# A scan kernel's first four steps: unit 1's state sums copied right behind step 0's k, and pieces of the weights taken up one place sooner

## The chip, the cores and the metric

One core of a Trainium2 chip runs the whole program. The metric is the device time in microseconds from the first to the last instruction; a profile of the same kernel has a span of its own, some tenths of a percent shorter. TensorE, VectorE, ScalarE, GpSimd and SyncE each work through a queue of their own in the order in which the program lists their instructions; semaphores hold an instruction back until what it needs is done. SyncE's queue issues nearly all transfers.

## The reference

A Mamba-2 scan is followed by a gated feed-forward block:

```python
# x: 4 sequences, 8 heads, 768 tokens, 32 wide; a: a decay per token; B, C: 16 wide
for c in range(nc):                       # chunks of the sequence
    L = exp(cum[:, :, :, None] - cum[:, :, None, :]) * causal
    y_intra = einsum('bhij,bhjd->bhid', einsum('bhin,bhjn->bhij', Cc, Bc) * L, xc)
    y_inter = einsum('bhin,bhnd->bhid', Cc, state) * exp(cum)[..., None]
    y[:, :, sl] = y_intra + y_inter
    state = decay_full * state + einsum('bhjn,bhjd->bhnd', Bc * decay_from_j, xc)
# y as (3072 tokens, 256)
h = y @ w_in            # 256 -> 2048
g = h * cos(h)
out = g @ w_out         # 2048 -> 256
```

The weights arrive as 64-bit floats and are used as 32-bit ones, so the kernel first puts the two 32-bit words of each number together.

## The kernel before, in words

The kernel cuts the sequences into chunks of 128 tokens (`NC` is 6). For each chunk it computes the scan's `y`, keeps it transposed in `yT`, and runs the feed-forward block over it in 16 steps (`NF`), each for 512 columns of hidden values: tokens of a part of the chunk by two groups of 128 hidden features. Chunk 0 is handled in two units of 64 tokens of every sequence, so that the first feed-forward steps can begin as soon as unit 0's `y` is there; step n of chunk 0 belongs to unit n mod 2.

A step consists of these pieces, each a short function:

- `first(n)` (L650): 8 matmuls of TensorE, `hp` from `w_in` and `yT`, into one PSUM bank. They are L663 in the profile.
- `wind_k(n)`: ScalarE rounds `hp`/2π to the integer `k` (L670). `wind_w(n)`: VectorE takes `w = hp/2π - k` (L676). `wind` is both.
- `gate(n)`: ScalarE turns `w` into the cosine (L685).
- `gated(n)`: VectorE multiplies `hp` by it into `gT` (L690); this is the last reader of `hp(n)`.
- `second(n)`: 8 matmuls of TensorE in chunk 0, `gT` by `w_out` into the accumulators `o` (L734).

The weights come in 16 pieces, `("in", 0..7)` and `("out", 0..7)`, each 512 KB of words. `grade` takes one up: ScalarE takes the absolute value of the high words (L231), GpSimd clamps it (L232), and ScalarE scales the low words (L229, the function `rest`, which with `later=True` is handed back and called afterwards). `join` finishes it: two VectorE instructions (L244, L246) and an addition on GpSimd (L254) that writes the piece into `w_in` or `w_out`. The tiles `mag` and `last` that lie between have three buffers each, the words eight. Steps 0 and 1 use pieces in 0 and out 0; steps 2 and 3 use in 1 and out 1; steps 4 and 5 use in 2 and out 2; steps 6 and 7 use in 3 and out 3.

The order on every engine is written out by hand. `first_steps` (L929) lists the steps 0 to 3 of chunk 0 along with the end of the scan of unit 1; from step 4 on, a loop does it: `first(n)`, `wind(n)`, the next piece's `grade`, `gate(n)`, the due `join`, `gated(n)`, parts of the next chunk's scan, and then `second(n - 2)`. The scan of the next chunk puts decay scans on VectorE (L510), one each in the steps 4, 6, 8 and 9; they read `arow`, a row of decays spread over all partitions by a DMA. `clips` computes what these DMAs read (`a_cut`, `a_all`), and SyncE's loads of chunk 1 come behind its two transfers.

PSUM, the accumulators' memory, is divided by tags with two buffers each: `"h"` and `"o"` of one bank, and `"scan"` of a pair of banks. A buffer goes to a new tile only when all readers of the old one are done. Chunk 0's scan uses `"scan"` for its matrices; `finish0(1)`, which runs in the middle of `first(0)`, takes both of them for unit 1's `y`. From each, ScalarE copies 256 columns of every partition to `yT` (L466). The first, `y[0]`, also holds unit 1's sums for the next state in other columns. The function `take_s1` copies these to `state` in two ScalarE instructions (L476); `add_s1`, at step 6, adds the old state to them on GpSimd. The steps 2 and 3 have `tag=None`, which means that their `hp` lies in a buffer of the tag `"scan"` (L652); the steps 0, 1 and those from 4 on use the tag `"h"`.

Of the kernel before, what the change touches and what calls it, by code (L numbers as in the profile page):

```python
# [25 lines left out]
def kernel(  # L26
# [42 lines left out]
    def bank(shape, name, tag):  # L69
        return psum.tile(shape, FP32, tag=tag, bufs=2, name=name)  # L70

    def pair(name):

        return psum.tile([P, 2, 4 * P], FP32, tag="scan", bufs=2, name=name)
# [120 lines left out]
    def kept(which, i):  # L195
        return (w_in[:, :, i * WC:(i + 1) * WC] if which == "in" else
                w_out[:, i * WF:(i + 1) * WF])
# [14 lines left out]
    def shares(which, ap, n):  # L212

        return [ap] if n == 1 else [ap.rearrange("p (k e f) -> p e k f", k=KT, e=n)[:, e]
                                    for e in range(n)]

    def grade(which, i, later=False, n=1):


        t = words.pop((which, i), None)  # L220
        if t is None:
            return
        mag = conv.tile([P, 2 * WC], FP32, tag="mag", bufs=3, name="mag")
        last = conv.tile([P, 2 * WC], U32, tag="last", bufs=3, name="last")
        low, high, mags, lasts = (shares(which, ap, n) for ap in (t[:, :, 0], t[:, :, 1], mag, last))
        held[which, i] = list(zip(high, shares(which, mag.bitcast(U32), n), lasts))

        def rest(e=0):
            ACT.activation(lasts[e], low[e], AF.Copy, scale=2.0 ** -29)  # L229
        for e in range(n):  # L230
            ACT.activation(mags[e], high[e].bitcast(FP32), AF.Abs)  # L231
            G.tensor_scalar(out=mags[e], in0=mags[e], scalar1=MOST, scalar2=LEAST,  # L232
                            op0=ALU.min, op1=ALU.max)
            if not later:
                rest(e)
        if later:
            return rest

    def join(which, i):


        parts = held.pop((which, i), ())
        for e, (high, bits, last) in enumerate(parts):
            V.tensor_scalar(out=bits, in0=bits, scalar1=3, scalar2=0x3FFFFFFF,  # L244
                            op0=ALU.logical_shift_left, op1=ALU.bitwise_and)
            V.scalar_tensor_tensor(out=bits, in0=high, scalar=0xC0000000, in1=bits,  # L246
                                   op0=ALU.bitwise_and, op1=ALU.bitwise_or)
            dst = kept(which, i)
            if len(parts) > 1:
                dst = dst[:, :, e * P:(e + 1) * P]  # L250
            else:
                bits, last = (ap.rearrange("p (k f) -> p k f", k=dst.shape[1])
                              for ap in (bits, last))
            G.tensor_tensor(out=dst.bitcast(U32), in0=bits, in1=last, op=ALU.add)  # L254
# [10 lines left out]
    for s in range(2):  # L265
# [3 lines left out]
        out=a_in, in_=a.rearrange("(u b) h (c p) -> (b h c) u p", u=NU, p=P))  # L269
# [91 lines left out]
    def weigh0(k):  # L361
        scs[k] = sc = scan.tile([P, 2 * H, N], FP32, tag="sc0", bufs=1, name="sc0")
        G.tensor_tensor(out=sc, in0=bs[:, k].rearrange("p q (h n) -> p (q h) n", h=H),
                        in1=lams[k].rearrange("p q h i -> p (q h) i")[:, :, W - 1:W]
                        .to_broadcast([P, 2 * H, N]), op=ALU.mult)
# [53 lines left out]
    def weights(k, q):  # L419

        m_of[k] = units[k]
        m, l = (ap[:, :, HH * q:HH * (q + 1)].rearrange("p s (k t) i -> p k s (t i)", k=2)
                for ap in (units[k], lams[k]))
        V.tensor_tensor(out=m, in0=gs[k, q][:, :, 0:2 * P].rearrange("p k (s i) -> p k s i", s=2),
                        in1=l, op=ALU.mult)
# [219 lines left out]
    def turn_of(n):  # L645

        c, f = divmod(n, NF)
        return (f % 2, f // 2) if c == 0 else divmod(f, NJ)

    def first(n, between=None, tag="h"):  # L650
        c, f = divmod(n, NF)
        hp[n] = bank([P, TB], "hp", tag) if tag else pair("hp")[:, 0]  # L652

        u, j = turn_of(n)
        if c == 0:
            to_, y = hp[n].rearrange("p (e i) -> p e i", e=2), yT[0][:, u]
        else:
            to_ = hp[n].rearrange("p (e t s i) -> p e t s i", e=2, t=2, s=2)
            y = yT[c].rearrange("p k (u s t i) -> p k u t s i", u=2, s=2, t=2)[:, :, u]
        for e in range(2):  # L660
            fs = slice((2 * j + e) * P, (2 * j + e + 1) * P)
            for k in range(KT):
                PE.matmul(to_[:, e], lhsT=w_in[:, k, fs], rhs=y[:, k],  # L663
                          start=(k == 0), stop=(k == KT - 1), skip_group_check=True)
            if between and e == 0:
                between()

    def wind_k(n):
        k = ffn.tile([P, TB], I32, tag="k", name="k")
        ACT.activation(k, hp[n], AF.Copy, bias=0.25, scale=INV_2PI)  # L670
        turns[n] = k

    def wind_w(n):
        k = turns[n]
        turns[n] = w = ffn.tile([P, TB], FP32, tag="w", name="w")
        V.scalar_tensor_tensor(out=w, in0=hp[n], scalar=INV_2PI, in1=k,  # L676
                               op0=ALU.mult, op1=ALU.subtract)

    def wind(n):
        wind_k(n)  # L680
        wind_w(n)

    def gate(n):
        cos = turns[n]
        ACT.activation(cos, cos, AF.Sin, bias=quarter, scale=TWO_PI)  # L685

    def gated(n):
        cos = turns.pop(n)
        gT[n] = ffn.tile([P, TB], FP32, tag="gT", bufs=LAG + 1, name="gT")
        V.tensor_tensor(out=gT[n], in0=hp.pop(n), in1=cos, op=ALU.mult)  # L690
        gT[n] = gT[n].rearrange("p (q m) -> p q m", q=4)
        if NF <= n < NC * NF - 1:
            differ(n)
# [29 lines left out]
    def second(n):  # L723
        c, f = divmod(n, NF)
        if c > 0:
            seven(n)
            return
        u, j = turn_of(n)
        if j == 0:
            o[c, u] = bank([P, 2, DM], "o", "o")  # L730
        g = gT.pop(n)
        for e in range(2):
            for t in range(2):
                PE.matmul(o[c, u][:, t], lhsT=g[:, 2 * e + t], rhs=w_out[:, 2 * j + e],  # L734
                          start=(j == e == t == 0), stop=(j == NJ - 1 and e == 1),
                          skip_group_check=True)
        if j < NJ - 1:
            return
        ob = conv.tile([P, 2, DM], FP32, tag="last", bufs=3, name="ob")
        ACT.copy(out=ob, in_=o[c, u])  # L740
        for p in range(2):
            nc.sync.dma_start(out=unit_rows[p, u], in_=ob[p * W:(p + 1) * W])
# [124 lines left out]
    def units_of_decay():  # L867
        G.tensor_copy(out=unit[:, 0:HH * P].rearrange("p (h i) -> p h i", h=HH),
                      in_=ident.unsqueeze(1).to_broadcast([P, HH, P]))
        G.tensor_copy(out=unit[:, HH * P:], in_=ident[:, 0:W])  # L870

    def clips():
        G.tensor_scalar(out=cut, in0=a_in, **clip)
        G.memset(cut[:, :, 0:1], 0.0)
        G.tensor_scalar(out=la, in0=a_in, **clip)
        for dst, src in ((a_cut, cut), (a_all, la)):
            nc.sync.dma_start(
                out=dst.rearrange("(u b) h (c p) -> (b h c) u p", u=NU, p=P), in_=src)
# [50 lines left out]
    def first_steps():  # L929

        weigh0(1)
        grade("in", 1)
        units_of_decay()
        for q in range(2):
            weights(1, q)
        states_of = []
        first(0, lambda: states_of.extend(finish0(1)))
        take_s1, add_s1 = states_of
        join("in", 1)
        wind(0)  # L940
        first(1)
        rest = grade("out", 0, later=True)
        clips()
        gate(0)
        rest()
        join("out", 0)
        gated(0)
        first(2, tag=None)
        wind(1)
        rest = grade("in", 2, later=True)  # L950
        gate(1)
        rest()
        join("in", 2)
        gated(1)
        first(3, tag=None)
        wind(2)
        rest = grade("out", 1, later=True)
        gate(2)
        rest()
        join("out", 1)  # L960
        second(0)
        gated(2)
        wind(3)
        second(1)
        rest = grade("in", 3, later=True)
        gate(3)
        take_s1()
        rest()
        join("in", 3)
        gated(3)  # L970
        grade("out", 2)
        return add_s1

    add_s1 = first_steps()
# [86 lines left out]
```

## Time and profile before

| | |
|---|---|
| time | 381.97 us, median of 3 runs (381.56 to 382.55) |
| span of the profile | 380.6 us, granted TensorE clock 0.990 |
| TensorE | 366.1 us busy, 96% of the span |
| VectorE | 280.3 us, 74% |
| GpSimd | 215.0 us, 56% |
| ScalarE | 172.6 us, 45% |
| data moved | 31.55 MB, 83 GB/s on average; 218 to 299 GB/s between 9.5 and 47.5 us |

In the digits of the profile's page each place is a fortieth of the span, 9.5 us; a digit is the busy share in tenths, and the row PEclk gives the clock that TensorE was granted, in tenths of full speed. In the timeline a line has its start in us, its length in us, engine, line of the code, operation, the tiles written and read, and the number of instructions that it merges; in brackets stands the idle time before it with what ended it. "issue" there means that nothing the profile shows held the engine back. `first_steps` takes place between 13 and 37 us; step 4 follows.

### The profile page before, as it was taken

How to read it: one execution, taken by the hardware profiler on the slowest of the kernel's cores; microseconds unless marked ns; L12 is line 12 of the kernel's file. 1: busy time of each engine (PE TensorE's matmuls, PEld its weight loads, DVE VectorE, ACT ScalarE, POOL GpSimd, SP SyncE). 2: the span in 40 equal slices, each digit the busy share in tenths (PEclk: the TensorE clock that was granted, in tenths of full speed). 3: DMA queues.
4: the chain of work that ended last, by engine and by line, in shares of the span. 5: the costliest groups of instructions: out<-in, count | busy, mean ns of one | idle time of the engine just before them, and what ended most of it. 6: DMA issues, size and time to landing. Idle time of an engine off the chain costs nothing.

```text
span 380.6 us, 8692 instructions
## 1 busy us (share of the span) xinstructions
PE 366.1 (96%) x3276; PEld 327.9 (86%) x3276; DVE 280.3 (74%) x471; ACT 172.6 (45%) x293; POOL 215.0 (56%) x334
## 2 busy tenths in 40 slices
PE   8929999999999999999999999999999999999996
PEld 4628887888989899999989999989999999999995
DVE  7672899989979966987775887875888782554543
ACT  3564666535335334434433444443444443434442
POOL 6563486459974553684354776344666434444551
PEclk9996999999999999999999999999999999999999
DMA  9988987315425732664222745121020010010011
GB/s 144 299 221 218 251 203 144 80 15 146 108 61 85 133 80 44 83 154 110 42 53 24 131 106 125 22 43 16 4 37 11 0 30 2 0 29 2 0 30 28
DMA packets 121354, 31.55 MB, mean 83 GB/s; under 512 B 90496, under 2 KB 117216, under 8 KB 121312
## 3 DMA queue, kind: packets, MB, share of 16 engines
q1 hardware_dynamic: 119024, 30.54, 37.4%
q10 hardware_dynamic: 2288, 0.46, 0.6%
q8 instruction: 26, 0.43, 0.5%
q14 instruction: 16, 0.13, 0.1%
HBM read 27.64 MB, written 3.34 MB: 81 GB/s over the span
## 4 chain that ended last, share of the span: by engine, by line
PE 78%; SPq 5%; DVE 5%; POOL 5%; DMA 3%; issue 2%; ACT 1%; POOLq 0%; ACTq 0%
PE hp L663 37%; PE o L772 30%; SPq L110 4%; PE y L602 3%; PE o L734 2%; PE g L560 2%; POOL words L709 2%; DMA bc<-in_C_dram 1%; PE y L595 1%; DMA arow<-a_cut 1%; DVE mag L246 1%; DVE gT L690 1%; DVE w L676 1%; DVE mag L244 1%; POOL gd L715 1%
## 5 line engine op out<-in xcount | busy, mean ns | idle before, releaser
L663 PE MATMUL hp<-yT,w_in 128*128 128x256 f32 x768 | 185.4, 385 | 8.2 <-DVE gT L690 6.2
L663 PEld LDWEIGHTS hp<-yT,w_in 128*128 128x128 f32 x768 | 140.5, 192 | 28.3 <-issue 10.8
L715 POOL TENSOR_TENSOR gd<-gT 128x256 f32<-128x256 f32 x79 | 59.0, 747 | 98.8 <-DVE gT L690 93.0
L685 ACT ACTIVATE w<-w,quarter 128x512 f32<-128x512 f32 x96 | 69.2, 721 | 77.5 <-DVE w L676 77.5
L676 DVE SCALAR_TENSOR_TENSOR w<-hp,k 128x512 f32<-128x512 f32 x96 | 65.4, 682 | 47.4 <-ACT k L670 47.3
L670 ACT ACTIVATE k<-hp 128x512 int32<-128x512 f32 x96 | 57.2, 596 | 89.7 <-PE hp L663 89.5
L690 DVE TENSOR_TENSOR gT<-hp,w 128x512 f32<-128x512 f32 x96 | 65.2, 679 | 33.0 <-ACT w L685 24.1
L772 PE MATMUL o<-words,gd 128*128 128x128 f32 x474 | 65.8, 275 | 0.0
L772 PEld LDWEIGHTS o<-words,gd 128*128 128x128 f32 x474 | 59.3, 192 | 0.0
L510 DVE TENSOR_TENSOR_SCAN lam<-arow,unit 128x512 f32<-128x512 f32 x40 | 56.5, 1411 | 0.0
L772 PEld LDWEIGHTS o<-w_out,gT 128*128 128x128 f32 x316 | 47.5, 191 | 4.0
L718 POOL TENSOR_TENSOR gd<-gT,gd 128x128 f32<-128x128 f32 x79 | 44.6, 565 | 6.2
L772 PE MATMUL o<-w_out,gT 128*128 128x128 f32 x316 | 48.0, 274 | 0.0
L717 POOL TENSOR_TENSOR gd<-gT,gd 128x128 f32<-128x128 f32 x79 | 44.0, 557 | 6.2
L734 PE MATMUL o<-w_out,gT 128*128 128x256 f32 x128 | 31.3, 390 | 0.0
L581 DVE TENSOR_TENSOR m<-g,lam 128x256 f32<-128x256 f32 x80 | 30.9, 415 | 0.5
L772 PE MATMUL o<-w_out,gd 128*128 128x128 f32 x158 | 30.6, 275 | 0.0
L772 PE MATMUL o<-words,gT 128*128 128x128 f32 x158 | 30.5, 275 | 0.0
L734 PEld LDWEIGHTS o<-w_out,gT 128*128 128x128 f32 x128 | 25.3, 198 | 3.7
L772 PEld LDWEIGHTS o<-w_out,gd 128*128 128x128 f32 x158 | 24.0, 192 | 0.0
L772 PEld LDWEIGHTS o<-words,gT 128*128 128x128 f32 x158 | 24.0, 192 | 0.0
L232 POOL TENSOR_SCALAR mag<-mag 128x512 f32<-128x512 f32 x16 | 11.6, 726 | 11.1 <-ACT mag L231 11.0
(108 smaller groups left out, 269.1 us busy)
## 6 DMA issues: line engine op xcount, KB each, us to landing
arow<-a_cut SPq DMA_DIRECT2D x20, 512.0 KB
words<-in_moe_w_in_dram SPq DMA_DIRECT2D x8, 512.0 KB
words<-in_moe_w_out_dram SPq DMA_DIRECT2D x8, 512.0 KB
out_dram<-sum SPq DMA_DIRECT2D x18, 128.0 KB
blocks<-in_B_dram SPq DMA_DIRECT2D x128, 8.0 KB
blocks<-in_C_dram SPq DMA_DIRECT2D x128, 8.0 KB
xr<-in_x_dram SPq DMA_DIRECT2D x14, 128.0 KB
along<-a_all SPq DMA_DIRECT2D x20, 64.0 KB
```

Of the source, the lines that this page charges most:

```text
L510: V.tensor_tensor_scan(out=lam[c, b][:, hs].rearrange("p h i -> p (h i)"), data0=rows_.rearrange("p h i -> p (h i)"), data1=unit[:, b % 2 ...
L581: V.tensor_tensor(out=m_[js, :, :, is_], in0=g_[js, :, :, is_], in1=l_[js, :, :, is_], op=ALU.mult)
L663: PE.matmul(to_[:, e], lhsT=w_in[:, k, fs], rhs=y[:, k], start=(k == 0), stop=(k == KT - 1), skip_group_check=True)
L670: ACT.activation(k, hp[n], AF.Copy, bias=0.25, scale=INV_2PI)
L676: V.scalar_tensor_tensor(out=w, in0=hp[n], scalar=INV_2PI, in1=k, op0=ALU.mult, op1=ALU.subtract)
L685: ACT.activation(cos, cos, AF.Sin, bias=quarter, scale=TWO_PI)
L690: V.tensor_tensor(out=gT[n], in0=hp.pop(n), in1=cos, op=ALU.mult)
L715: G.tensor_tensor(out=d[:, 0:2], in0=g[:, 1:2].to_broadcast([P, 2, P]), in1=g[:, 3::-3], op=ALU.subtract)
L717: G.tensor_tensor(out=d[:, 2], in0=g[:, 0], in1=d[:, 0], op=ALU.subtract)
L718: G.tensor_tensor(out=d[:, 3], in0=g[:, 2], in1=d[:, 2], op=ALU.subtract)
L734: PE.matmul(o[c, u][:, t], lhsT=g[:, 2 * e + t], rhs=w_out[:, 2 * j + e], start=(j == e == t == 0), stop=(j == NJ - 1 and e == 1), skip_gr ...
L772: PE.matmul(at[q], lhsT=a_[q], rhs=w[q], start=(j == 0 and q in starts), stop=(j == NJ - 1), skip_group_check=True)
```

## The change

The change rewrites the order inside `first_steps` and nothing else; no instruction is added or removed. It has four parts.

1. `take_s1()` moves from behind `gate(3)` to right behind step 0's `wind_k`, so that the buffer with the state sums becomes free before the steps 2 and 3 ask for theirs.
2. Each piece of weights from out 0 to out 2 is taken up one place sooner: out 0 ahead of `first(0)` instead of behind `first(1)`, in 2 in step 0 instead of step 1, and so on; out 2, which was taken up at the end of `first_steps`, is taken up in step 3.
3. The joins of out 0 and out 1 move up: out 0's two VectorE instructions stand between `wind_k(0)` and `wind_w(0)`, out 1's between `first(3)` and `wind(2)`. Those of in 2 and in 3 stay where they were.
4. `clips()` comes behind `gate(0)` instead of ahead of it; on GpSimd it now follows the clamp of in 2 instead of that of out 0.

```diff
+        rest = grade("out", 0, later=True)
         states_of = []
         first(0, lambda: states_of.extend(finish0(1)))
         take_s1, add_s1 = states_of
+        rest()
         join("in", 1)
-        wind(0)
+        wind_k(0)
+        take_s1()
+        join("out", 0)
+        wind_w(0)
         first(1)
-        rest = grade("out", 0, later=True)
+        rest = grade("in", 2, later=True)
+        gate(0)
         clips()
-        gate(0)
         rest()
-        join("out", 0)
         gated(0)
         first(2, tag=None)
         wind(1)
-        rest = grade("in", 2, later=True)
+        rest = grade("out", 1, later=True)
         gate(1)
         rest()
         join("in", 2)
         gated(1)
         first(3, tag=None)
+        join("out", 1)
         wind(2)
-        rest = grade("out", 1, later=True)
+        rest = grade("in", 3, later=True)
         gate(2)
         rest()
-        join("out", 1)
         second(0)
         gated(2)
         wind(3)
         second(1)
-        rest = grade("in", 3, later=True)
+        rest = grade("out", 2, later=True)
         gate(3)
-        take_s1()
         rest()
         join("in", 3)
         gated(3)
-        grade("out", 2)
         return add_s1
```

## The prediction

> **What bounds the kernel now.** I read the page first: the engines' shares, and the digits of TensorE and its clock.
>
> ```profile
> PE 366.1 (96%) x3276; PEld 327.9 (86%) x3276; DVE 280.3 (74%) x471; ACT 172.6 (45%) x293; POOL 215.0 (56%) x334
> ...
> PE   8929999999999999999999999999999999999996
> ...
> PEclk9996999999999999999999999999999999999999
> ```
>
> TensorE is the bound: 366.1 of 380.6 us. It has one real hole, the third slice (19 to 28.5 us), and right behind it the only slice in which its clock is granted at 0.6. Both lie in the steps that the change rewrites, so I cut that stretch into windows (after the length: PE, PEld, DVE, ACT, POOL busy, granted clock, DMA share, GB/s):
>
> ```profile
> 20.00:24.00 4.00, 1.85 (x8) 1.13 (x6) 2.65 (x5) 3.33 (x7) 3.32 (x6) 1.00 0.89 261
> 24.00:28.80 4.80, 0.00 (x0) 0.01 (x1) 3.78 (x7) 2.25 (x4) 2.42 (x3) 0.92 0.74 150
> 28.80:37.00 8.20, 8.18 (x24) 6.75 (x25) 2.41 (x4) 4.10 (x8) 2.39 (x3) 0.63 0.87 232
> 37.00:45.00 8.00, 8.00 (x38) 7.04 (x38) 5.36 (x7) 3.92 (x7) 3.73 (x5) 1.00 0.90 279
> ```
>
> TensorE does nothing from 24 to 28.8 us, then works 8.2 us on 24 matmuls at clock 0.63; afterwards it does 38 in 8.0 us. The timeline says what ended the hole:
>
> ```profile
> 27.99 0.68 DVE L690 TENSOR_TENSOR gT<-hp,w 128x512 f32<-128x512 f32 x1
> ...
> 28.82 3.75 PE L663 MATMUL hp<-yT,w_in 128*128 128x256 f32 x8 [5.16 <-DVE gT L690]
> ...
> 32.37 4.85 PE L734 MATMUL o<-w_out,gT 128*128 128x256 f32 x16
> ...
> 34.65 0.61 ACT L476 ACTIVATE state<-y,slot 128x128 f32<-128x128 f32 x2
> ...
> 37.05 1.89 PE L663 MATMUL hp<-yT,w_in 128*128 128x256 f32 x8
> ...
> 38.78 1.89 PE L734 MATMUL o<-w_out,gT 128*128 128x256 f32 x8
> ```
>
> The matmuls at 28.82 are first(3). They wait for the gT at 27.99, gated(2), the last reader of hp(2). There are two buffers with the tag "scan". finish0(1) fills both: y[1] is free after the yT copies, but y[0] holds unit 1's state sums until take_s1 (L476), which ScalarE reaches only at 34.65. So hp(2) gets y[1]'s buffer, none is left for hp(3), and first(3) waits until hp(2) is consumed. This one late copy explains hole and slow clock. After 37.05 TensorE waits for a named engine only 1.4 us in total (1.0 for gT, 0.4 for a memset), and the last of the chain is its matmuls: what is won before 37.05 should reach the end.
>
> **What the skill says.** "TensorE: Matmul & The Clock Gate", "What's actually happening": an idle window of about 3.4 us halves TensorE's clock, until about as long a busy one. The trace agrees: 5.16 us idle, then 0.63; the hole of 1.80 us at 20.2 us left 1.00. The same page's table of specifications: ScalarE, VectorE and GpSimd are strict FIFOs, so a waiting instruction holds all behind it. "DMA: Bandwidth & Descriptors", "Anatomy of one DMA": about 2 us fixed, most of it the receipt after the last byte. Here a piece whose last packets ran at 11.5 us was read at 13.09 without a wait, so at most 1.6 us. "Runtime: NRT & Kernel Launch", "Instruction fetch mechanics": instructions come in blocks of 256. Between the starts after TensorE's two "issue" holes, at 15.58 and 21.99, lie some 127 matmuls with as many weight loads, which fits.
>
> **The change, part by part.**
>
> *take_s1 behind wind_k(0).* Same two copies, 0.50 us of ScalarE's queue (34.65 to the next start at 35.15), now between k(0) and sin(0). k(0) starts at 18.28, so y[0] is free at about 19.4, before first(2) starts (its first matmul runs at 19.8). Both buffers are free in time and first(3) follows first(2) directly.
>
> TensorE's sum: first(2) ends at 23.66 (start 21.99, 1.67 long). Then first(3), second(0), second(1), 8 matmuls each: 8 take 1.73 at full clock (37.05 to 38.78). 23.66 + 3 x 1.73 = 28.85 for first(4), against 37.05: **8.2 us**, of which 5.2 is the hole and 3.0 the slow clock (8.2 busy against 5.2).
>
> Are their inputs there? I lay the new queues out with spacings from the timeline: on ScalarE k 0.49, abs 0.57, sin 0.63, last 0.57; on VectorE w 0.61, join 0.45 + 0.61, gT 0.61; on GpSimd clamp 0.61, add 1.27.
>
> ```profile
> 17.08 0.65 ACT L466 COPY yT<-y 128x256 f32<-128x256 f32 x2 [2.72 <-PE y L457]
> ...
> 18.28 0.60 ACT L670 ACTIVATE k<-hp 128x512 int32<-128x512 f32 x1 [0.55 <-PE hp L663]
> ...
> 21.99 1.67 PE L663 MATMUL hp<-yT,w_in 128*128 128x256 f32 x7 [1.80 <-issue]
> ```
>
> ScalarE: k(0) 18.3, copies 18.8, abs(in 2) 19.3, sin(0) 19.85, last 20.5, k(1) 21.0, abs(out 1) 21.5, sin(1) after w(1) 22.4, last 23.0, k(2) after first(2) 23.7, abs(in 3) 24.2. VectorE: gated(0) to 21.3, w(1) to 22.35, join(in 2) to 23.4, gated(1) to 24.0, join(out 1) to 25.1, w(2) to 25.7; sin(2) to 26.5, gated(2) to 27.2; w(3) from 27.55, join(in 3) to 29.3, gated(3) to 30.0 (before: 36.3). TensorE needs gT(0) at 25.4, gT(1) at 27.1, gT(2) at 30.6, gT(3) at 34.0: slack of 3 us or more. Weights: the adds of out 0 end near 19.6, in 2 near 24.7, out 1 near 26.4, in 3 near 30.6; needed at 25.4, 28.85, 30.6 and 35.8.
>
> *out 0 before finish0(1).* Its abs now stands ahead of the yT copies, a new wait on the path: behind it in ScalarE's queue are the copies, first(1) waits for them, and GpSimd's clamp stands ahead of add(in 1), which first(2) needs. Has out 0 landed? Packets of 2 KB, 256 a piece and counted in order, put its end at 15.0 us. Low bound no delay: abs at 15.0. High bound with 2 us of receipt: abs 17.0 to 17.6, copies 0.6 us late at 18.3, where first(1) wants them at 18.2; add(in 1) ends at 19.6, first(2)'s first matmul comes at 19.8. I take 0 and keep 0.5 for the range.
>
> *The other pieces one place sooner.* Nothing added: the same abs, clamp, joins and copies on the same engines, ahead of waits. out 2's moves out of the end of first_steps, where it stood ahead of k(4). By the same count in 2, out 1, in 3 and out 2 end at 16.5, 18.0, 19.3 and 20.7, at least 2 us before their abs. The three buffers each of mag and last suffice: at most two pieces are open, and the add that frees the third comes earlier. 0.
>
> *wind_w(0) behind join(out 0).* Those joins (1.1 us) fit between VectorE's 16.75 and k(0)'s end at 18.88. Bounds 0 and 0.3, hidden.
>
> *clips behind gate(0).* The cut waits for clamp(in 2): a_cut goes out at about 21.5 instead of 21.04, and SyncE's loads of chunk 1 start 0.5 us later. They run at a DMA share of 0.8 to 0.9 and get no faster, while their users come 8.2 us sooner. Counted from packets, step 4's scan finds arow at 30.1 + 0.5 + at most 2 = 32.6 where it starts at 42.17 - 8.2 = 34.0; abs(out 3) 31.3 + 2.5 = 33.8 against 34.7; abs(in 6) 42.0 + 2.5 = 44.5 against 45.1. All fit, by 0.6 us at the least. 0, with 1 us in the range.
>
> **After step 4.** VectorE is full from 39.61 to about 67 us, and first(12) waits 0.39 us for it at 65.78. It is a second bound of the stretch and must start as much earlier: w(4) follows k(4), that follows first(4): 28.85 + 1.73 + hand-over and k, 31.3 against 39.61, 8.3 us. VectorE is free at 30.0. So the phase between the two is kept and the gain passes through. Sum: 381.97 - 8.2 = **373.8 us**.
>
> **Rivals.**
>
> *A, the fetch hole at 20.2 us closes too.* It is 1.80 us; without it first(4) comes at 27.0, gain 10.0, 372.0. Against: TensorE's order and the DMA traffic up to 20 us are unchanged, and the fetch's packet shows at 19.5 us. 12%.
>
> *B, the start goes faster than what feeds it.* A late arow or word piece, or joins stretched beside GpSimd (0.98 to 1.25 instead of 0.69 or 0.43 occur), puts VectorE back 1 to 3 us, and first(12) passes it on. Gain 5.2 to 7.2, some 376. For: the thin margins of 0.6 to 1.4 us. Against: the landings hold 2 us of receipt where 1.6 or less was seen. 20%.
>
> *C, the wait comes back in another place.* If out 0's abs or the join ahead of w(0) waited for data until about 27 us, the copies, first(1) and first(2) behind them would come 10 us late: 381.97 + 10 - 8.2 = 383.8, slower than before. For: two new places ahead of a strict queue. Against: out 0's packets are through at 15.0. 3%; as much again for gains under 5 us.
>
> *The forecast*, 7.3 to 9 us: 62%.
>
> **How the numbers follow.** 373.8 is the likeliest case. Down to 371.8 the range takes in A; up to 376.8 it takes in B and the bounds of the unknown waits (0.5 + 0.3 + 1). 0.3% is 1.1 us: only C and part of the small gains fall short. Faster 0.95, same 0.02, slower 0.03.
>
> **What would show it.** first(3) directly behind first(2) near 23.7 us, no wait of TensorE for gT there, clock 1.00 from 24 to 37 us, L476 near 18.8, first(4) near 28.9, VectorE's w(4) near 31.3. Wrong if yT's copies (L466) start later than 17.7, if VectorE idles for a DMA between 30 and 60 us, or if TensorE waits anew near 57 us.

## The result, and the profile after

| | before | after |
|---|---|---|
| time | 382.20 us, median of 4 (381.56 to 382.55) | 377.25 us, median of 4 (376.24, 376.62, 377.88, 378.01) |
| span of the profile, granted clock | 380.6 us, 0.990 | 374.5 us, 0.999 |
| VectorE, busy | 280.3 us | 282.5 us |

The ratio is 0.9871, with a 95% interval of 0.9839 to 0.9903: 4.95 us faster, where 8.2 was forecast. The time lies 0.45 us above the range's upper end of 376.8. The same kernel on another chip (`e5` below) took 376.42 us, 5.7 us less than the kernel before, so the size of the shortfall itself varies.

The profile's page after, the same three rows as before:

```profile
PE 364.1 (97%) x3276; PEld 325.7 (87%) x3276; DVE 282.5 (75%) x471; ACT 172.0 (46%) x293; POOL 213.6 (57%) x334
...
PE   7979999999999999999999999999999999999995
...
PEclk9999999999999999999999999999999999999999
```

The slice with the slow clock is gone. The windows of the kernel after, cut as before (PE, PEld, DVE, ACT, POOL busy, granted clock, DMA share, GB/s):

```profile
20.00:24.00 4.00, 2.02 (x10) 1.65 (x9) 2.79 (x6) 2.91 (x6) 2.82 (x6) 1.00 0.74 272
24.00:28.80 4.80, 4.80 (x24) 4.21 (x24) 4.15 (x6) 2.83 (x5) 3.02 (x3) 1.00 0.62 98
28.80:37.00 8.20, 8.20 (x40) 7.22 (x39) 7.54 (x10) 6.56 (x12) 5.87 (x7) 1.00 1.01 279
37.00:45.00 8.00, 7.90 (x37) 6.67 (x36) 7.76 (x12) 5.07 (x9) 5.94 (x7) 1.00 0.74 192
```

From 24 to 28.8 us TensorE does 24 matmuls instead of none, and from 28.8 to 37 us 40 instead of 24. So the hole and the slow clock are both gone, as intended. But the VectorE column has grown to 7.54 of 8.20 and 7.76 of 8.00: a second engine is now nearly as full as TensorE. The timeline of the kernel after shows how both come to step 4:

```profile
17.11 0.69 ACT L231 ACTIVATE mag<-words 128x512 f32<-128x512 f32 x1 [2.47 <-DMA words<-in_moe_w_out_dram]
17.69 0.65 ACT L466 COPY yT<-y 128x256 f32<-128x256 f32 x2
...
18.46 1.27 POOL L254 TENSOR_TENSOR w_in<-mag,last 128x512 uint32<-128x512 uint32 x1
18.53 1.48 DVE L244 TENSOR_SCALAR mag<-mag 128x512 uint32<-128x512 uint32 x1 [1.21 <-POOL mag L232]
18.79 0.62 ACT L670 ACTIVATE k<-hp 128x512 int32<-128x512 f32 x1
19.26 0.66 ACT L476 ACTIVATE state<-y,slot 128x128 f32<-128x128 f32 x2
...
20.66 0.68 DVE L676 SCALAR_TENSOR_TENSOR w<-hp,k 128x512 f32<-128x512 f32 x1
...
22.30 3.40 PE L663 MATMUL hp<-yT,w_in 128*128 128x256 f32 x15 [1.98 <-issue]
...
25.77 1.12 DVE L244 TENSOR_SCALAR mag<-mag 128x512 uint32<-128x512 uint32 x1
...
27.54 0.68 DVE L676 SCALAR_TENSOR_TENSOR w<-hp,k 128x512 f32<-128x512 f32 x1
...
28.99 1.89 PE L663 MATMUL hp<-yT,w_in 128*128 128x256 f32 x8
...
32.04 0.68 DVE L690 TENSOR_TENSOR gT<-hp,w 128x512 f32<-128x512 f32 x1
...
32.64 0.68 DVE L676 SCALAR_TENSOR_TENSOR w<-hp,k 128x512 f32<-128x512 f32 x1
```

TensorE is where the sum put it: L476 frees the buffer at 19.3, first(3) follows first(2) in one group of 15 matmuls at 22.30, and first(4) starts at 28.99, 8.06 us sooner than before. VectorE is not. w(0) starts at 20.66 instead of 18.91. It stands behind out 0's join, whose abs waited until 17.11 for its words, and whose first instruction took 1.48 us beside GpSimd's add. w(4) starts at 32.64 without a wait, right behind gT(3) at 32.04; the forecast had gT(3) end at 30.0 and w(4) at 31.3. VectorE's own lead at step 4 is 39.61 - 32.64 = 6.97 us.

What happens to the 1.1 us between the two leads? These windows run 30 us from each kernel's w(4). Before:

```profile
39.61:49.61 10.00, 10.00 (x48) 8.79 (x48) 9.71 (x14) 6.87 (x12) 6.09 (x6) 1.00 0.93 249
49.61:59.61 10.00, 10.00 (x48) 8.81 (x47) 9.93 (x12) 5.95 (x11) 8.96 (x10) 1.00 0.86 207
59.61:69.61 10.00, 9.61 (x57) 7.74 (x62) 9.90 (x16) 7.39 (x14) 4.72 (x6) 1.00 0.49 90
```

After:

```profile
32.64:42.64 10.00, 9.90 (x46) 8.42 (x45) 9.72 (x15) 7.53 (x13) 7.39 (x7) 1.00 0.86 220
42.64:52.64 10.00, 9.83 (x47) 8.33 (x46) 9.93 (x12) 5.03 (x10) 9.07 (x10) 1.00 0.89 231
52.64:62.64 10.00, 9.29 (x51) 7.33 (x56) 9.90 (x16) 7.46 (x14) 4.61 (x6) 1.00 0.96 213
```

VectorE is as full in both (the third number behind the length), so nothing can be caught up there. TensorE, which had been full, now has gaps. The timeline after names them (the last, before step 12, was there before as well):

```profile
46.93 1.97 PE L663 MATMUL hp<-yT,w_in 128*128 128x256 f32 x8 [0.17 <-DVE gT L690]
...
54.40 1.97 PE L663 MATMUL hp<-yT,w_in 128*128 128x256 f32 x8 [0.32 <-DVE gT L690]
...
58.92 1.32 PE L663 MATMUL hp<-yT,w_in 128*128 128x256 f32 x5 [0.39 <-DVE gT L690]
```

TensorE hands its surplus back in waits for VectorE: its own lead, by the starts of first(n), is 8.06 us up to step 6, 7.39 at step 9 and 6.86 from step 11 on. From here on, the lead is measured by the start of gT(n), before minus after. It is 6.87 us at step 4, 6.86 at steps 12 and 32, 6.52 at step 36, 6.57 at the last step, and 6.1 at the end of the span.

### The profile page after: what moved, and what is told of

It is laid out like the page before. It is cut to its first block, busy times and chain, and to the rows that moved or that the text cites. A ratio compares the mean times of both kernels' runs of the same rounds, so it can differ in the third digit from the quotient of the medians.

```text
span 374.5 us, 8693 instructions
## 1 busy us (share of the span) xinstructions
PE 364.1 (97%) x3276; PEld 325.7 (87%) x3276; DVE 282.5 (75%) x471; ACT 172.0 (46%) x293; POOL 213.6 (57%) x334
## 4 chain that ended last, share of the span: by engine, by line
PE 70%; DVE 13%; POOL 6%; issue 4%; DMA 3%; SPq 1%; ACT 1%; DVEq 0%; POOLq 0%; ACTq 0%
PE hp L663 34%; PE o L772 30%; POOL words L709 3%; DVE mag L246 3%; PE y L602 2%; DVE mag L244 2%; DVE w L676 2%; DVE gT L690 2%; DMA words<-in_moe_w_out_dram 2%; PE g L560 2%; DVE lam L510 2%; PE y L595 1%; DMA bc<-in_B_dram 1%; POOL gd L715 1%; DVE m L581 1%
## 5 line engine op out<-in xcount | busy, mean ns | idle before, releaser
L663 PEld LDWEIGHTS hp<-yT,w_in 128*128 128x128 f32 x768 | 139.1, 190 | 24.5 <-issue 6.9
L772 PEld LDWEIGHTS o<-w_out,gT 128*128 128x128 f32 x316 | 47.5, 191 | 4.0
L717 POOL TENSOR_TENSOR gd<-gT,gd 128x128 f32<-128x128 f32 x79 | 44.0, 557 | 6.2
L718 POOL TENSOR_TENSOR gd<-gT,gd 128x128 f32<-128x128 f32 x79 | 42.6, 539 | 6.2
L734 PE MATMUL o<-w_out,gT 128*128 128x256 f32 x128 | 30.1, 379 | 0.0
L734 PEld LDWEIGHTS o<-w_out,gT 128*128 128x128 f32 x128 | 24.2, 190 | 3.3
L789 DVE TENSOR_TENSOR sum<-ps,sum 128x256 f32<-128x256 f32 (+1 forms) x27 | 16.7, 644 | 0.6
```

The source lines that it names most:

```text
L663: PE.matmul(to_[:, e], lhsT=w_in[:, k, fs], rhs=y[:, k], start=(k == 0), stop=(k == KT - 1), skip_group_check=True)
L717: G.tensor_tensor(out=d[:, 2], in0=g[:, 0], in1=d[:, 0], op=ALU.subtract)
L718: G.tensor_tensor(out=d[:, 3], in0=g[:, 2], in1=d[:, 2], op=ALU.subtract)
L772: PE.matmul(at[q], lhsT=a_[q], rhs=w[q], start=(j == 0 and q in starts), stop=(j == NJ - 1), skip_group_check=True)
```

## The experiments

The theory from these traces, V: from step 4 to about step 12 VectorE bounds the kernel, so the end follows VectorE's w(4), and what put w(4) back is work of VectorE ahead of w(0) and w(2). The rivals: the end follows TensorE and the shortfall arises later; the pieces' new places are the gain, or a plain loss; part of the gain is lost to the hole at 20 us. The kernel before was run beside each group: 382.22 us beside the runs e1 to e4, 382.14 beside e5 to e8, 382.16 beside e9 to e11, 382.43 beside e12.

### Part 1 alone, and the rest alone

`e1_take_alone`, against the kernel before:

```diff
-        wind(0)
+        wind_k(0)
+        take_s1()
+        wind_w(0)
...
         gate(3)
-        take_s1()
```

> The kernel before with one edit: take_s1 behind wind_k(0), all pieces of weights and clips at their old places. Theory V (what reaches the end is VectorE's lead at w(4); in the changed kernel it was cut to 6.9 us by out 0, whose abs waited for its words until 17.1 us and whose joins, 1.48 us long beside GpSimd, held w(0) back to 20.7 us): w(0) back at about 18.9 us, first(4) near 28.9, w(4) near 31.5, some 374.5 us, at least 1.5 us faster than the changed kernel's 377.25. Rival L (chunk 1's loads, which start late, pace the steps 4 to 10): clips and loads start at their old times, so also faster, 374 to 375, but with w(0) irrelevant. Rival S (the pieces one place sooner are needed, since without them VectorE's and ScalarE's queues are longer in steps 1 to 3): 378 or more.

Measured: 377.40 us (376.12 to 381.67), ratio 0.9882 (0.9843 to 0.9922). Part 1 alone gains as much as the whole change, within the intervals, but the gain over the changed kernel that V expected didn't come. w(0) started at 19.10, as V wanted. In this profile the hole at 20 us came out longer, though, and the clock fell behind it. The windows of this run:

```profile
24.00:28.80 4.80, 4.80 (x16) 3.91 (x15) 3.44 (x7) 3.75 (x8) 2.27 (x3) 0.65 0.68 115
```

And its timeline:

```profile
22.72 5.08 PE L663 MATMUL hp<-yT,w_in 128*128 128x256 f32 x15 [2.35 <-issue]
...
31.10 1.89 PE L663 MATMUL hp<-yT,w_in 128*128 128x256 f32 x8
...
33.65 0.69 DVE L676 SCALAR_TENSOR_TENSOR w<-hp,k 128x512 f32<-128x512 f32 x1 [1.08 <-ACT k L670]
```

After 2.35 us of idling the clock fell (a mean of 0.65 in this window) while first(2) and first(3) ran, first(4) came at 31.10, and here w(4) waits for TensorE, by way of k(4). The lead of 5.96 at step 4 then fell to 4.16 at step 43, which no theory had foreseen.

`e3_pieces_alone`, against the changed kernel: the other three parts without the first.

```diff
-        take_s1()
         join("out", 0)
...
         gate(3)
+        take_s1()
```

> The changed kernel with take_s1 back behind gate(3): only the pieces, joins and clips moved. Both theories: first(3) again waits for gated(2), which in the changed kernel's order ends about 1 us later than before, the clock drops again, and the time is 382 to 384 us; no gain from the pieces by themselves.

Measured: 383.51 us (382.49 to 384.63), ratio 1.0029 (1.0015 to 1.0043), as expected: slower than before. Its timeline:

```profile
30.03 3.47 PE L663 MATMUL hp<-yT,w_in 128*128 128x256 f32 x8 [5.28 <-DVE gT L690]
...
35.58 0.61 ACT L476 ACTIVATE state<-y,slot 128x128 f32<-128x128 f32 x2
...
36.78 1.89 PE L663 MATMUL hp<-yT,w_in 128*128 128x256 f32 x8
...
154.71 0.60 ACT L670 ACTIVATE k<-hp 128x512 int32<-128x512 f32 x1 [0.64 <-PE hp L663]
```

The hole of 5.28 us is back along with the late L476, and first(3) comes 1.2 us later than before (28.82). In this profile that isn't yet a loss: the slow clock behind the hole lasted 3.4 us where it lasted 6.8 before, so first(4) comes at 36.78 and gT(4) 0.2 us sooner than before. The loss comes later, in two places. The last line is k(34), before which ScalarE idles 0.64 us; before, it idles 0.36:

```profile
154.63 0.60 ACT L670 ACTIVATE k<-hp 128x512 int32<-128x512 f32 x1 [0.36 <-PE hp L663]
```

Step 34 loses 0.3 us so, and the end of the span another 0.4. Both are lost in every profile with the pieces moved (after, e2 to e6, e8 to e10, e12) and in none with the old order (e1, e7, e11). So the pieces' new places cost some 0.75 us late in the program, by something other than the first steps. At the median e3 is 1.3 us slower than before; the rest of that may be the later first(3), which this profile doesn't show.

### What holds VectorE back

`e2_join_behind_w`, against the changed kernel:

```diff
         take_s1()
-        join("out", 0)
         wind_w(0)
+        join("out", 0)
```

> The changed kernel with out 0's join behind wind_w(0) instead of ahead of it; clips and all loads as in the changed kernel. Theory V: w(0) at about 19.5 us instead of 20.7, gT(0) at 21.1 instead of 22.1, w(4) about 1.0 to 1.2 us sooner, 376.1 us. Rival L: loads unchanged, so 377.2 us.

Measured: 378.95 us (376.07 to 380.19), ratio 0.9892 (0.9859 to 0.9925): missed. Its timeline says why V's number failed:

```profile
19.58 0.69 DVE L676 SCALAR_TENSOR_TENSOR w<-hp,k 128x512 f32<-128x512 f32 x1 [1.98 <-ACT k L670]
...
25.57 1.48 DVE L244 TENSOR_SCALAR mag<-mag 128x512 uint32<-128x512 uint32 x1 [0.39 <-POOL mag L232]
...
27.70 0.68 DVE L676 SCALAR_TENSOR_TENSOR w<-hp,k 128x512 f32<-128x512 f32 x1
```

w(0) came 1.1 us sooner, but w(2) no sooner than with the whole change (27.54). The join of out 1 stands ahead of it, again with an L244 stretched to 1.48 us. So there are two joins in the way, and moving one buys nothing at w(4) (32.78). And again most of the lead was lost about step 42: 6.42 before it, 3.89 at step 43 and 2.64 from step 48 on; behind the wait TensorE's clock stood at 0.50 from 186.1 to 189.6 us.

`e4_light_vector`, against the changed kernel, takes work off VectorE in the steps 4 to 8. It leaves out VectorE's two join instructions for each of the pieces out 2 and in 4, so the upper bits of those weights are not put together.

```diff
-            V.tensor_scalar(out=bits, in0=bits, ...)
-            V.scalar_tensor_tensor(out=bits, in0=high, ...)
+            if (which, i) not in (("out", 2), ("in", 4)):
+                V.tensor_scalar(out=bits, in0=bits, ...)
+                V.scalar_tensor_tensor(out=bits, in0=high, ...)
```

> The changed kernel without the two VectorE instructions in the joins of the pieces out 2 and in 4 (steps 4 and 5): the upper bits of these two pieces are not merged, the rest of the computation is unchanged. Some 2.2 us less work for VectorE between 33 and 38 us, nothing else moved. Theory V: VectorE's lead over the kernel before grows from 6.9 to 8 us or more by step 5, TensorE no longer waits for gT near 47 and 58 us, and its 8.1 us lead of first(4) reaches the end: about 376.0 us. Rival L: the loads are as before, 377.2 us.

Measured: 379.68 us (376.96 to 380.34), ratio 0.9912 (0.9882 to 0.9943). The time missed, but the trace did what V says: with 2.1 us less work on VectorE (280.4 us busy against 282.5), the lead grew to 8.07 at step 5 (TensorE's own was 8.25), and 7.86 of it still stood at step 12. At step 42 it was 7.57, at step 43 5.90, and the table of waits of this run has the reason (its helper has one line more, so L525 here is L524 elsewhere):

```profile
DVE turned L525 <- DMA blocks<-in_C_dram: 1.6, 1, 1.6
```

### The second limit: the queue that issues the loads

That wait is on a transfer, and in e2 it is longer. The timeline of e2:

```profile
181.26 0.41 DVE L524 STREAM_TRANSPOSE turned<-blocks 128x256 f32<-128x256 f32 x1
...
184.09 0.45 DVE L524 STREAM_TRANSPOSE turned<-blocks 128x256 f32<-128x256 f32 x1 [2.42 <-DMA blocks<-in_C_dram]
...
185.53 1.09 PE L560 MATMUL g<-cT,turned 32*64 32x256 f32 x32 [1.93 <-ACT cT L544]
```

The blocks come so late because SyncE issues one transfer after another. Its instructions in the timeline of before, with start and length:

```profile
105.16 2.28 SPq L155 DMA_DIRECT2D blocks<-in_C_dram  x4
111.32 0.36 SPq L164 DMA_DIRECT2D arow<-a_cut  x1
...
153.15 3.77 SPq L110 DMA_DIRECT2D bc<-in_B_dram  x6
```

And of after:

```profile
105.28 2.28 SPq L155 DMA_DIRECT2D blocks<-in_C_dram  x4
107.65 0.42 SPq L164 DMA_DIRECT2D arow<-a_cut  x1
...
150.26 3.78 SPq L110 DMA_DIRECT2D bc<-in_B_dram  x6
```

Before, SyncE rests from 107.44 to 111.32. After, it goes on at 107.65: it has work on hand the whole time, and at 150 us it leads by 2.9 us where the engines lead by 6.5. In e2 it leads by 0.25 (152.90). The compute engines run up against a queue that can't start sooner by as much as they do. The loads at 150 us, of B and x for the chunk after next, aren't urgent; they only stand ahead of the blocks.

The second group of runs asks this question. `e5_after_again` is the changed kernel as it is. `e6_loads_later` puts those loads behind step 11 of their chunk; `e7_before_loads_later` does the same to the kernel before:

```diff
-            if c > 0 and f == (NJ if c == 1 else 0):
+            if c > 0 and f == (NJ if c == 1 else 11):
```

> The changed kernel itself, run again beside the next three. Theory B (behind VectorE's lead stands a second limit: SyncE's queue has no idle time from about 108 to 180 us, so the blocks of chunk 3's second unit do not come sooner, and step 42's transposes wait for them in some executions and not in others): times spread from 376 to 379 us, median 377.3. Rival H (the spread is TensorE's clock, which drops in some executions behind the instruction-fetch hole at 20 us): the same times, but then the next kernel spreads as much.

> The changed kernel with one edit in the loop: from chunk 2 on, the loads of B and x for the chunk after next are issued at the chunk's step 11 instead of its step 0. That takes 12 transfers, some 7.7 us of SyncE's queue, from ahead of the blocks of chunk 3's second unit. Theory B: no wait of VectorE for blocks near 180 us, the lead of 6.6 to 6.9 us reaches the end in every execution: 376.2 us, spread under 1 us. Rival H: as the changed kernel, 377.3 us with the same spread.

> The kernel before with the same edit of the loop's loads. Theory B: the kernel before has its blocks in time (its step 42 comes 6.6 us later), so nothing changes: 382.2 us. Rival (the loads' place costs time by itself): other than that by 1 us or more.

Measured: e5 376.42 us (376.01 to 377.01), ratio 0.9851 (0.9829 to 0.9873), lower and tighter than I expected of it. e6 376.18 (375.75 to 377.28), 0.9852 (0.9827 to 0.9877). e7 381.87 (381.14 to 382.97), 0.9997 (0.9984 to 1.0011), no change, as expected. In e6's timeline the blocks are there when VectorE comes, two transposes in one go:

```profile
182.09 0.74 DVE L524 STREAM_TRANSPOSE turned<-blocks 128x256 f32<-128x256 f32 x2
```

The lead at step 42, and what was lost of it by step 48, tells the runs apart: with the loads in their old place e1 lost 1.77, e2 3.78, e4 1.68, e5 0.46 and the first profile of after 0.0; with the loads later, e6 and the five kernels below that share the edit all lost 0.0 (5.58 to 5.60 in e6). So SyncE's queue is a real second limit. Its price in time can't be told from e5 and e6, which ran on the same chip (0.24 us between medians whose runs overlap): there the changed kernel lost little, while e1, e2 and e4 ran on another chip. At a granted clock of 0.997 or more, e5's five executions have a median of 376.37 and e6's three of 375.80, which fits the 0.46 that e5's profile lost there. e6's spread of 1.5 us wasn't expected: its two executions of 377.2 and 377.3 have a clock of 0.995, as the rival with the clock would have it, so both limits are at work.

### Both joins out of the way, and the hole as well

`e8_joins_and_loads`: e6 with both joins behind the step's own work.

```diff
-        join("out", 0)
         wind_w(0)
+        join("out", 0)
...
-        join("out", 1)
         wind(2)
+        join("out", 1)
```

> The changed kernel with the loads later and with the joins of out 0 and out 1 behind wind_w(0) and wind(2) instead of ahead of them. Theory V (what sets VectorE's lead is that these joins, stretched beside GpSimd, hold w(0) and w(2) back): w(0) near 19.6 us, w(2) near 25.1 instead of 27.5, gated(3) near 30, w(4) near 31.8 instead of 32.6, set by first(4) and no longer by gated(3); VectorE's lead 7.8 us instead of 6.9, about 375.2 us. Rival (w(4) is set by ScalarE or TensorE anyway): lead 6.9, 376.2 us.

Measured: 375.47 us (375.13 to 377.66), ratio 0.9841 (0.9813 to 0.9869). Compared at a granted clock of 0.997 or more, its four executions took 375.13 to 375.57 and e6's three 375.75 to 376.18: about 0.5 us for the joins. It is faster than the kernel before, its median is 0.95 us below e5's on the same chip, and it is the lowest of all here; but two of its six executions (377.29 and 377.66, at a clock of 0.994 to 0.995) lie above all of e5's. Its profile caught an execution with a hole of 3.07 us and the slow clock behind it, so w(4) is late there (34.15).

The hole can be moved, if it is the border of a block of instructions, as the prediction read it: 44 tiny calls at the start (88 matmuls and as many weight loads on a bank that nobody reads) then shift every border in TensorE's program. `e9_all_and_shift` is e8 with these, `e10_after_shift` is e6 with them, and `e11_take_shift` is e1 with them and with the loads later.

```diff
-    fill(bank([P, 2, P], "warm", "o"), 1)
+    warm = bank([P, 2, P], "warm", "o")
+    fill(warm, 1)
+    for i in range(44):
+        at_q = slice(32 * (i % 4), 32 * (i % 4) + 32)
+        PE.matmul(warm[at_q, 0, 0:16], lhsT=ones[0:W, 0:32], rhs=ones[0:W, 0:16], ...)
```

> The kernel with joins behind w and loads later (e8), with 44 very small calls of TensorE (88 matmuls with their weight loads, 176 instructions, on ones, into a scratch bank) ahead of its first real work, where it waits anyway. They move the borders of the 256-instruction blocks: the border that fell on first(2)'s second matmul falls in first(4) instead. Theory F (the hole near 20 us is the wait for the next block of TensorE's instructions; where it ends late, the clock drops too and first(4) slips from 29 to 31 us): no hole of 1.7 us or more between 19 and 24 us, granted clock 0.997 or more in every execution, first(3) done before 24.5 us, w(2) near 24.5, w(4) near 31; spread under 1 us; 374.5 us against e8's 375.5. Rival (the hole is a missing operand, such as in 1's addition or a PSUM buffer): hole and clock drops as before, 375.5 us.

> The changed kernel with the loads later (e6) and the same 44 small calls; the joins where the change puts them. Theories F and V together: no hole, no clock drop, but w(2) is held at about 27.3 us by join(out 1) all the same, so w(4) stays near 32.5 and VectorE's lead at 7: 376.0 us in every execution. If the hole had set VectorE's lead: 374.5 us.

> take_s1 alone (e1) with the loads later and the same 44 small calls: of the change only part 1. Theory V: pieces one place sooner give nothing by themselves. With the old order out 0's abs stands behind k(0) and its join behind w(0); gated(3) near 31.5 us, w(4) near 32.2, lead 7.3 us, 375.7 us, at least as fast as e10. If the pieces' earlier places help once hole and loads are out of the way: 376.5 us or more.

Measured: e9 376.10 us (375.67 to 377.05), ratio 0.9845 (0.9822 to 0.9868); e10 376.68 (376.55 to 378.42), 0.9870 (0.9846 to 0.9894); e11 376.95 (376.85 to 377.17), 0.9865 (0.9842 to 0.9888). All three missed the time expected of them: the calls take 1.33 us, and first(0) starts at 15.0 to 15.2 us, where it starts at 13.6 to 14.5 in the profiles without them. What they show is the mechanism. The timeline of e9:

```profile
17.96 6.31 PE L663 MATMUL hp<-yT,w_in 128*128 128x256 f32 x28
...
25.30 0.67 DVE L676 SCALAR_TENSOR_TENSOR w<-hp,k 128x512 f32<-128x512 f32 x1
...
27.56 1.89 PE L663 MATMUL hp<-yT,w_in 128*128 128x256 f32 x8
```

28 matmuls run in a row, the hole is gone, w(2) is at 25.30 instead of 27.54, and first(4) comes 9.5 us sooner than before. A set of profiles now exists in which TensorE and VectorE lead by different amounts (starts of first(4) and w(4), each taken from before's 37.05 and 39.61):

| profile | TensorE's lead, first(4) | VectorE's lead, w(4) | lead at step 4's gT | at step 12's | at the span's end |
|---|---|---|---|---|---|
| after | 8.06 | 6.97 | 6.87 | 6.86 | 6.1 |
| e1 | 5.95 | 5.96 | 5.96 | 5.95 | 4.1 |
| e5 | 7.99 | 7.23 | 7.12 | 7.12 | 5.9 |
| e6 | 5.92 | 5.86 | 5.86 | 5.86 | 5.1 |
| e8 | 5.52 | 5.46 | 5.46 | 5.45 | 4.7 |
| e9 | 9.49 | 7.54 | 7.44 | 7.46 | 6.7 |
| e10 | 8.99 | 6.66 | 6.56 | 6.55 | 5.8 |
| e11 | 8.46 | 6.13 | 5.57 | 5.54 | 5.5 |

In e1, e6 and e8 a slow clock held TensorE back, and the two engines' leads are the same to 0.06 us, so these three don't tell them apart. In the other five TensorE leads by 0.8 to 2.3 us more, and what is left at step 12 is VectorE's lead: to 0.1 us in four, while e11 falls short by a further half microsecond at step 4, where VectorE waits for the clamp of out 2. e10 gains 0.9 us on TensorE over after and loses 0.3 at the lead, for w(4) was 0.3 later. e9 and e10 differ in the joins alone: 0.88 us at w(4), 0.88 at the lead, 0.9 at the span's end, 0.6 between the medians. e10 and e11 differ in the parts 2 to 4 of the change: 0.5 us at w(4) and 1.0 at the lead in favour of the pieces taken up sooner, of which the two late losses seen in e3 leave 0.3 at the span's end; the times (376.68 and 376.95) don't part them.

`e12_best` is e9 without the second warming matmuls, `fill(warm, 1)`, to win the start back.

> e9 without the second of the two warming calls at the start (0.85 us), since the 44 small calls keep TensorE busy in its place. The computation is unchanged. Theories V and F: the scan's first matmul comes at about 4.3 us instead of 5.2, all of the start with it by 0.8 us, no hole, no clock drop; VectorE's lead some 8 us instead of 7.2; 375.0 us, faster than the changed kernel (376.4 beside the kernel before) and than e8. Rival (the start is set by the transfers of C and x, which do not move): as e9, 376 us.

Measured: 375.99 us (375.85 to 377.47), ratio 0.9840 (0.9813 to 0.9867): missed. Its timeline:

```profile
4.37 4.38 PE L346 MATMUL a_ps<-m,those 128*64 128x256 f32 x20
```

These 20 matmuls start 0.8 us sooner than in e9, as expected, but take 4.38 us instead of 2.38: with half of the warming gone, the early scan eats what was saved. That a slow clock is the reason is likely but not shown; the clock's record begins only at 8.5 us here.

## Why the prediction fell short

**Right.** The cause (the late copy holds a buffer of the tag "scan") and its cure: e1 alone gives the gain, and e3 without it is slower than before. TensorE's sum: first(4) at 28.99, predicted 28.85. The clock of 1.00 from 24 to 37 us. Luck had a part in both: e6 has the same first steps, its hole was 0.2 us longer, the clock fell, and first(4) came at 31.13. No early wait of any size for chunk 1's loads: a_cut went out at 23.39, later than the 21.5 predicted, yet VectorE was full from w(4) on. Of the three signs of being wrong, the wait of TensorE near 57 us appeared (54.40), and the copies' start lay at its limit (17.69). Rival A didn't happen: the hole of 1.98 us at 20.3 stayed, and e9 and e10 show that even without it the end would not have followed.

**Wrong, first term: out 0 and its join were costed at nothing.** The prediction took 0 for "out 0 before finish0(1)" and called the joins ahead of w(0) "Bounds 0 and 0.3, hidden". Three things were mis-sized.

- The landing. By the prediction's own count of packets, those of out 0 end at 15.4 us in the kernel after; its abs started at 17.11, 1.7 us later. I had derived at most 1.6 us from another piece, kept 2 us as the high bound and taken 0. The Trainium skill, "DMA: Bandwidth & Descriptors", "Anatomy of one DMA", has about 2 us, but for transfers that GpSimd issues, while SyncE issues these. In the other profiles with the piece in this place the same count gives 0.4 to 2.6 us, so it is no constant here. yT's copies moved from 17.08 to 17.69 and k(0) from 18.28 to 18.79: 0.51 us.
- The join. Its L244 takes 0.42 us where no add runs (23.82 in the kernel after) but 1.48 beside GpSimd's add. The Trainium skill, "SBUF — State Buffer", "SBUF: two separate sides", says that VectorE and GpSimd share a pair of ports, and that of a GpSimd instruction and a VectorE instruction in a mode that needs the pair, whichever starts first keeps it for the whole instruction. That L244 runs in such a mode isn't shown here, but the traces fit: the add began at 18.46 and ended at 19.73, L244 began at 18.53 and ended at 20.01, 0.28 us behind it; out 1's L244 ended at 26.89, 0.28 us behind an add that ended at 26.61. In e5 it is 19.80 after 19.51. In all three L244 waits the add out. Ahead of w(0) and w(2) the change puts the join just where the previous piece's add runs, and k(0), done at 19.41, waits until 20.66. The prediction saw such stretches, but laid its queues out with 0.45.
- The second join. out 1's join ahead of w(2) was an entry of 1.1 us in my list of VectorE's queue, from 24.0 to 25.1, and w(2) was to start then. It ran from 25.77 to 27.54, 1.8 us late by the first two things and 0.7 us longer, and w(2) started at 27.54; gT(2) 29.01, w(3) 30.08, and gT(3) ends at 32.7 instead of 30.0.

Together this made w(4) 1.3 us late against the predicted 31.3. That the joins have a share in it is shown by e8 against e6 and e9 against e10, which differ in them alone: 0.5 to 0.6 us in the times. The 0.9 us at w(4) between the single profiles of e9 and e10 isn't theirs alone, for out 0's abs started 0.7 us later in e10 (17.37 against 16.71). The landing's share is read from the trace alone. The step that failed is the one that let "the phase between the two" be kept: VectorE wasn't free at 30.0, and as it was the bound of the next stretch, TensorE's 8.06 shrank to 6.87. That is rival B by name ("joins stretched beside GpSimd"), with its 5.2 to 7.2 us and "some 376", to which I gave 20%.

**Wrong, second term: what is won at the start was taken to reach the end.** I checked the loads up to step 9 and no further. SyncE's queue is full up to 180 us after the change, and whether step 42's blocks come in time differs from execution to execution: 0 to 3.8 us were lost there in the profiles, and 0 wherever the loads were put off. The two higher times of the changed kernel (377.88 and 378.01, about 1.5 us above the other two at the same clock of 0.999 to 1.000) would fit this, but it isn't shown, and it isn't the only candidate: e10 has two such times (377.70 and 378.42, at a clock of 0.997 and 0.998) with the loads put off.

**Wrong, third term: "Nothing added" for the other pieces one place sooner.** The two late losses, 0.3 us at step 34 and 0.4 at the end, go with the pieces' new places in every profile. The second lies behind the last outputs' transfers: SyncE's wait for them ends 2.4 us behind VectorE's last instruction in both kernels, and the closing instructions of GpSimd then end 0.4 us later. The cause of both stays open. In the new order ScalarE has three waiting instructions more (114 against 111 in the trace) and GpSimd three fewer (114 against 117), so all that follows in their programs stands at another place; a block border would fit, and no run tests it.

**The sum for the profiled execution.** 8.2 predicted; 6.9 left at step 12, as w(4) came 1.3 late; 6.6 at the last step, behind the 0.3 at step 34; 6.1 at the span's end. The median gain of 4.95 is some 1.2 us less, mostly because the profiled execution of the kernel after is its fastest (376.24).

## What to carry to other kernels

When a hole of the busiest engine is closed, work out the start of the next-busiest engine behind it just as carefully: the gain that arrives is the smaller of the two leads, and "it has slack" must be checked with the real length of each instruction at its new place. A VectorE instruction like L244, which was seen to wait a GpSimd instruction out, should be costed with the rest of that instruction wherever the two meet. A schedule that gets faster by several microseconds also runs up against the queue that issues its loads: look for where that queue's last gap lies before promising that the gain reaches the end.

## What the hardware showed that I had not expected

- TensorE's clock fell after shorter holes than I had thought, and not by their length alone. Holes at 20 us of 1.70 to 2.13 us (before, after, e2 to e5, e7) left 1.00 behind them; those of 2.17 (e6), 2.35 (e1) and 3.07 us (e8) were followed by 3.41 us at 0.50, a mean of 0.65 to 0.76 in the window from 24 to 28.8 us. The Trainium skill, "TensorE: Matmul & The Clock Gate", "What's actually happening", has an idle window of about 3.4 us and calls it free-running. The stretches between the changes of the clock fit such a grid (3.41, 6.83, 17.07 and 23.89 us are 1, 2, 5 and 7 times 3.41), but the window need not be idle throughout: in the one ahead of e6's drop, from 20.28 to 23.69 us, TensorE was busy for 1.24 us. So it is in part chance whether a hole of about 2 us costs anything. A drop moved first(4) from about 29.0 to 31.1 or more, and w(4) by 1 us or more.
- The fetch of a block of instructions isn't hidden here. In ten profiles, before's among them, TensorE resumes 2.3 to 2.5 us after the packet of the instruction queue starts, so the hole's length depends on when that packet comes (19.6 to 21.0 us); 176 added instructions removed it from its place.
- Eight transfers of blocks in a row keep SyncE's queue for 4.60 us or more (up to 5.24), some 0.58 us each, and this is what fills it. The Trainium skill, "DMA: Bandwidth & Descriptors", "Issuing engines are not separate DMA queues", calls the time to initiate a DMA usually small against the DMA itself; with many DMAs of 8 KB, as here, the sum of these times is what the loads wait for.
